# Row pairs for the upper half of the spectral weights, in a fused attention and spectral-mixing kernel

## The chip, the cores and the metric

The kernel runs on one core of a Trainium2 chip. The metric is the device time of one execution in microseconds, lower being better. TensorE (PE) multiplies matrices, with a separate unit that loads its weights (PEld); VectorE (DVE) and ScalarE (ACT) read PE's results from PSUM; GpSimd (POOL) here mainly issues transfers, and SyncE (SP) issues the stores of the output. Sixteen DMA engines carry out all transfers.

## The reference

The inputs are float32. `q`, `k` and `v` have 8 batches, 8 heads, 576 positions and 64 elements; `f` has one forget gate for each batch, head and position. Causal attention with a decay from the gates gives `x` of 8 x 576 x 512. Then the 64 lowest frequencies of `x` along the positions are multiplied by one complex 512 x 512 matrix per frequency ("mode"), and the result is transformed back and mixed.

```python
log_f = np.log(np.clip(f, 0.0001, 1.0)); cum = np.cumsum(log_f, axis=-1)
scores = scale * np.matmul(q, k.transpose(0, 1, 3, 2))
decay = cum[:, :, :, None] - cum[:, :, None, :]
attn = softmax(np.where(causal, -1000000000.0, scores + decay))
x = np.matmul(attn, v)            # then (B, S, H * D)
X = np.fft.rfft(x, axis=1)
Xr, Xi = (np.real(X[:, :n_modes]), np.imag(X[:, :n_modes]))
Yr = np.einsum('bmd,mde->bme', Xr, w_r) - np.einsum('bmd,mde->bme', Xi, w_i)
Yi = np.einsum('bmd,mde->bme', Xr, w_i) + np.einsum('bmd,mde->bme', Xi, w_r)
Y[:, :n_modes] = Yr + 1j * Yi
u = x + np.fft.irfft(Y, n=S, axis=1)
return u + np.maximum(u @ w_ch, 0.0)
```

`w_r` and `w_i` are 64 matrices of 512 x 512 each, 134 MB together, and all of them are read once.

## The kernel before

**Weights and units.** A unit is four modes (`NU` = 16 units). The 512 rows `d` of a unit's matrices come in four tiles, numbered by `dc`, each of 128 partitions and 1 MB in bf16. The transfers convert float32 to bf16, and so POOL issues them. For `dc` 0 and 1 a tile holds 128 rows (0 to 127, or 128 to 255) of both `w_r` and `w_i`, with one row on each partition; it is loaded in two halves, one for each of the two matrices (L156), and each contiguous run is one row of 512 numbers. For `dc` 2 and 3 a tile holds rows 256 to 511 of `w_r` (2) or `w_i` (3), with two neighbouring rows on each partition ("row pairs"), and a contiguous run is two rows (L165). `issue_w` loads the tiles in the order of `wseq`: first the list `early`, then the rest by unit. `issue_half` loads half a tile. Tiles lie in the pool `wpool` of seven buffers, used in turn, except for a few "guests" that lie in space of `x_all` or `yx` that is free at that time. A load waits until the product that read the buffer before has been computed.

**Two phases.** The first phase is a loop over 32 pairs of heads (`g` 0 to 3, and batch `b` within each), with two iterations more to drain it. Iteration `i` issues the loads of `q` and `k` for pair `i + 4`, half a weight tile, the load of `v` for pair `i + 3`, and another half tile (except where `i` is in `less`). Then PE, DVE and ACT work on the scores of pair `i` and on the values of pair `i - 1`: transposes of `q` and `k` (`tp`), scores (`sps`, `s`), transposes of the scaled values (`vn` on DVE, `tv`, `vT`, `vp`), products with the values (`pav`), and the normalization into `x_all`. The order of instructions on each engine is the order of the program (`manual_schedule`). At the end of iteration `i` stands `dft(i - 2)`, the spectrum of pair `i - 2`: five matmuls with the position blocks of `x_all` as weights and a basis of 3 x 64 columns (`bas3`). For `g` of 0 and 1 (pairs 0 to 15, iterations 2 to 17) the result is copied to `XS`, with one row `d` on each partition; for `g` of 2 and 3 it is two groups of five matmuls, with every second row as weights, and the result goes to `XP`, which has row pairs on the partitions.

**Early products.** From iteration 10, `spec_early` multiplies one tile of `early` by the spectrum, one at the end of each iteration and a second one in iterations 10 to 13. It takes eight matmuls into a PSUM tile `A0`, four at a time in different column groups. For `dc` 0 ACT copies the result to `yacc` in `yx`; for `dc` 1 DVE adds it there. `early` has 28 entries: `dc` 0 of all 16 units, then `dc` 1 of units 0 to 11. PSUM tiles with the tag `m` (transposes, spectrum, early products and others) take turns in two buffers.

**Second phase.** It goes through the units, with the tiles that are left (`dc` 2 and 3, and from unit 12 on `dc` 1 too). Each product frees a buffer, and POOL issues the next load after it. Beside this the kernel computes `x @ w_ch` (`pxw`), and folds the first 12 units back into `x` (`fold`). After the last tile the rest is folded, and the output is computed and stored.

The weight operands of the products are slices like these, for `dc` 0 and 1, and for 2 and 3:

```python
lhsT, rhs = XS[:, dc, c0 : c0 + 32], w8[:, n, j, :]
lhsT, rhs = XPv[:, c0 : c0 + M, m], w8[:, j, n, :]
```

## Time and profile before

| what | value |
|---|---|
| three runs, median (lowest to highest) | 437.75 us (437.21 to 437.8) |
| the profiled execution: its time, its span | 436.43 us, 434.6 us |
| PE, DVE, ACT, POOL busy | 343.3, 267.9, 234.1, 145.0 us |
| the loop's end (first product of the second phase) | 232.75 us |
| landing of the last weight tile | 402.1 us |
| 1024 KB load, issue to landing (median) | 29.5 us (`w_r`), 31.7 us (`w_i`) |
| 512 KB load, issue to landing (median) | 11.1 us (`w_r`), 12.3 us (`w_i`) |
| bytes read from HBM, written | 163.73 MB, 9.44 MB |

Times inside the execution are counted from the start of the span. The page cuts the span into 40 slices of 10.9 us; a digit is the busy share of a slice in tenths. The DMA row is the mean share of the 16 DMA engines. In the DMA view "share" is the sum of the packets' own times over 16 engines' time, and it is above 100 % when an engine has more than one packet under way. A row of a timeline has the start in us, the duration in us, the engine, the line, the operation with its tiles, the count, and in brackets the idle time before it and what ended it. A row of the chain of waits has the start, the duration, the engine, the tile, the line and the count.

### The profile page before, as it was taken

The numbers are of one execution on the slowest core, as the hardware profiler recorded it, in microseconds if no ns is written. First come the engines' busy times: TensorE is split into PE (matmuls) and PEld (weight loads), VectorE is DVE, ScalarE is ACT, GpSimd is POOL, SyncE is SP. The second block draws the span as 40 slices with busy tenths as digits, with TensorE's granted clock in tenths as the row PEclk, the third lists the DMA queues.
The fourth block names the chain that finished last, engine by engine and source line by source line (L and its number), as shares of the span: only waits on it lengthen the run. The fifth ranks groups of instructions, "written<-read, shape, count | busy, mean of one in ns | idle before, by whom it ended". The sixth has DMA issues, their size and how long they took to land.

```text
span 434.6 us, 10304 instructions
## 1 busy us (share of the span) xinstructions
PE 343.3 (79%) x4264; PEld 189.6 (44%) x4274; DVE 267.9 (62%) x651; ACT 234.1 (54%) x358; POOL 145.0 (33%) x215
## 2 busy tenths in 40 slices
PE   1689787798898898988896386599877498888993
PEld 1455555554555565555553142244433233334330
DVE  6677888877778778888885122222233165565794
ACT  4556777687887766656660022024322166564783
POOL 6544445444544353444213211111122202110273
PEclk9986999999999999999999579589999699999998
DMA  8999999999999999999999999999999999998498
GB/s 185 205 233 220 233 219 232 225 227 233 231 229 227 226 228 225 228 225 228 227 218 213 212 212 211 212 212 213 211 212 212 209 209 211 210 209 158 168 383 323
DMA packets 68543, 96.76 MB, mean 223 GB/s; under 512 B 3728, under 2 KB 45200, under 8 KB 68496
## 3 DMA queue, kind: packets, MB, share of 16 engines
q0 software_dynamic: 62800, 85.64, 106.3%
q1 hardware_dynamic: 5696, 10.47, 6.6%
q8 instruction: 33, 0.54, 0.4%
q14 instruction: 14, 0.11, 0.1%
HBM read 163.73 MB, written 9.44 MB: 398 GB/s over the span
## 4 chain that ended last, share of the span: by engine, by line
DMA 43%; PE 31%; DVE 18%; issue 3%; ACT 3%; POOL 1%; DVEq 0%; POOLq 0%
DMA w<-in_moe_w_r_dram 22%; DMA w<-in_moe_w_i_dram 20%; PE pav L477 5%; DVE vT L384 4%; DVE qkT L360 4%; DVE x_all L492 4%; PE A L194 4%; PE sps L432 3%; PE tv L382 3%; PE pd L521 3%; PE vp L393 2%; DMA qk<-in_k_dram 2%; PE Z L654 2%; DVE vn L372 2%; PE U L654 2%
## 5 line engine op out<-in xcount | busy, mean ns | idle before, releaser
L439 ACT ACTIVATE et<-sps 128x1024 bf16<-128x1024 f32 x96 | 96.0, 1049 | 13.9 <-PE sps L432 11.5
L477 PE MATMUL pav<-vs,et 128*128 128x65 bf16 (+1 forms) x896 | 52.1, 198 | 0.2 <-DVE vn L372 0.2
L360 DVE COPY qkT<-tp 128x640 bf16<-128x640 bf16 x64 | 48.7, 763 | 2.8 <-PE tp L355 2.8
L815 DVE TENSOR_TENSOR Yb<-A,yx 128x512 bf16<-128x512 f32 x15 | 10.4, 691 | 61.0 <-PE A L194 60.9
L477 PEld LDWEIGHTS <-et 128*128 128x128 bf16 (+1 forms) x896 | 37.2, 103 | 17.9 <-issue 13.6
L432 PE MATMUL sps<-qkT 64*128 64x512 bf16 (+4 forms) x320 | 39.8, 312 | 1.1 <-DVE qkT L360 1.1
L194 PE MATMUL A<-w,XP 128*16 128x512 bf16 (+1 forms) x240 | 21.9, 449 | 23.0 <-DMA w<-in_moe_w_i_dram 12.8
L694 PE MATMUL pxw<-wch,xT 128*128 128x512 bf16 (+1 forms) x152 | 39.0, 402 | 0.9 <-issue 0.3
L492 DVE TENSOR_TENSOR x_all<-pav,rcp 128x384 bf16<-128x384 f32 (+2 forms) x96 | 36.2, 377 | 3.3
L355 PE MATMUL tp<-ident_bf,qk 128*64 128x128 bf16 x576 | 30.3, 237 | 9.3 <-DMA qk<-in_k_dram 9.3
L384 DVE COPY vT<-tv 128x576 bf16<-128x576 bf16 x32 | 24.2, 757 | 19.8 <-PE tv L382 19.8
L165 POOL DMA_DIRECT2D w<-in_moe_w_r_dram x16 | 11.9, 743 | 71.8 <-PE A L194 50.5
L701 ACT CAST XW<-pxw 128x512 bf16<-128x512 f32 (+1 forms) x16 | 9.4, 585 | 47.3 <-PE pxw L694 47.3
L156 POOL DMA_DIRECT2D w<-in_moe_w_r_dram x27 | 20.5, 758 | 38.7 <-DMA w<-in_moe_w_i_dram 9.4
L404 ACT COPY vs<-vp 128x576 bf16<-128x576 bf16 x32 | 20.5, 640 | 21.7 <-PE vp L400 21.7
L165 POOL DMA_DIRECT2D w<-in_moe_w_i_dram x19 | 13.3, 698 | 53.3 <-PE A L194 31.6
L701 ACT CAST yx<-pxw 128x512 bf16<-128x512 f32 (+1 forms) x24 | 14.0, 585 | 31.4 <-PE pxw L694 31.4
L109 POOL DMA_DIRECT2D qk<-in_q_dram x32 | 19.5, 610 | 32.5 <-PE sps L432 6.2
L741 ACT CAST x_all<-pu 128x512 bf16<-128x512 f32 (+1 forms) x40 | 23.4, 584 | 11.2 <-PE pu L740 10.3
L491 DVE RECIPROCAL rcp<-pav 128x6 f32<-128x6 f32 (+2 forms) x96 | 16.2, 169 | 17.4 <-PE pav L477 17.3
L156 POOL DMA_DIRECT2D w<-in_moe_w_i_dram x27 | 20.3, 752 | 18.4 <-DMA w<-in_moe_w_i_dram 8.2
L109 POOL DMA_DIRECT2D qk<-in_k_dram x32 | 19.2, 601 | 19.3 <-DMA w<-in_moe_w_i_dram 5.2
(149 smaller groups left out, 677.8 us busy)
## 6 DMA issues: line engine op xcount, KB each, us to landing
w<-in_moe_w_r_dram POOLq DMA_DIRECT2D x16, 1024.0 KB, 29.5
w<-in_moe_w_i_dram POOLq DMA_DIRECT2D x15, 1024.0 KB, 31.7
w<-in_moe_w_r_dram POOLq DMA_DIRECT2D x27, 512.0 KB, 11.1
w<-in_moe_w_i_dram POOLq DMA_DIRECT2D x27, 512.0 KB, 12.3
out_dram<-o_sb SPq DMA_DIRECT2D x36, 256.0 KB, 3.2
vt<-in_v_dram POOLq DMA_DIRECT2D x29, 288.0 KB, 10.7
qk<-in_q_dram POOLq DMA_DIRECT2D x32, 144.0 KB, 10.8
qk<-in_k_dram POOLq DMA_DIRECT2D x32, 144.0 KB, 10.4
```

What stands on the lines that cost most here:

```text
L109: nc.gpsimd.dma_start(qk[64 * n : 64 * n + 64, :, :], src[b, 2 * g : 2 * g + 2, :, :].rearrange("h (p r) d -> p h (r d)", p=64),)
L156: nc.gpsimd.dma_start(w8[:, t, :, :], src[4 * u : 4 * u + 4, dc * 128 : (dc + 1) * 128, :].rearrange("m p e -> p m e"),)
L165: nc.gpsimd.dma_start(w8[:, j : j + step, :, :].rearrange("p m r e -> p m (r e)"), src[m : m + step, 256:512, :].rearrange("m (p r) e -> p ...
L194: nc.tensor.matmul(A[32 * j : 32 * j + M, :], lhsT=lhsT, rhs=rhs, start=st_, stop=sp_)
L355: nc.tensor.transpose(tp[64 * hp : 64 * hp + 64, r - r0, :, :].rearrange("p n c -> p (n c)"), qk[:, hp, r * 64 : r * 64 + 64], ident_bf[:, :],
L360: nc.vector.tensor_copy(st[i]["T"][:].rearrange("p n (c r) -> p n c r", r=9)[:, :, :, r0:r1], tp[:, 0 : r1 - r0, :, :].rearrange("p r n c ...
L384: nc.vector.tensor_copy(st[i]["vT"][:].rearrange("p (c r) -> p c r", r=9), tv[:].rearrange("p r c -> p c r"))
L432: nc.tensor.matmul(ps[:, hp, c : c + n], lhsT=KT[sl, jb * 128 : jb * 128 + 128], rhs=QT[sl, i0 : i0 + n], start=True, stop=True,)
L439: nc.scalar.activation(st[i]["et"][:, T, :, :], ps[:], ACT.Exp, scale=scale)
L477: nc.tensor.matmul(pav[:Ms, sb % 3, hp, :], lhsT=eblk(i, hp, jb, sb), rhs=rhs, start=(jb == 0), stop=(jb == sb),)
L492: nc.vector.tensor_tensor(x_all[:ns, g, b, lo:hi, :].rearrange("p s (h d) -> p s h d", h=2), pav[:ns, lo % 3 : lo % 3 + n, :, 0:Dh], _stri ...
L694: nc.tensor.matmul(pxw[rows, :], lhsT=xT[:, eb, sb * 128 : sb * 128 + Ms], rhs=wch[:, eb, :], start=(eb == 0), stop=(eb == NEB - 1),)
```

## The change

For units 8 to 15, the tiles of `dc` 0 and 1 take the form that `dc` 2 and 3 have: `dc` 0 is rows 0 to 255 of `w_r` and `dc` 1 the same rows of `w_i`, in row pairs on 128 partitions. Their contiguous runs in HBM are two rows, 4096 B in float32. Units 0 to 7 keep the old form (`by_rows`). Halves of the new tiles are two modes each; in the second phase such a tile is one transfer.

The spectrum of rows 0 to 255 is therefore made in two forms: for the modes of units 0 to 7 as before into `XS` (now half as long), and for the modes of units 8 to 15 by row pairs into the new tile `XQ`. For pairs 0 to 15 `dft` issues three groups of five matmuls with 96 columns each, in place of one group with 192, and two ACT copies in place of one.

Because `dc` 0 of a unit from 8 on needs the spectrum of all 16 pairs of `g` 0 and 1, the order of `early` changes: `dc` 0 of units 0 to 7, `dc` 1 of units 0 to 7, then `dc` 0 of units 8 to 15 and `dc` 1 of units 8 to 11. The second product per iteration stands in iterations 10, 11, 18, 19 and 20, and iteration 16 has none. Tiles 16 and 17 of the sequence (units 8 and 9, `dc` 0) become guests in `yx`.

```diff
--- before.py
+++ after.py
@@ -50,7 +50,9 @@
     KL = 2 * NM - KF
     NW = 7
     NX = 12
-    XROW = 24 * NM + 32
+    NL = 8
+    ML = 4 * NL
+    XROW = 24 * ML + 32
     scale = 1.0 / math.sqrt(Dh)
     TWO_PI_OVER_S = 2.0 * math.pi / S
     NEAREST = 1.5 * 2.0**23
@@ -66,6 +68,7 @@
     x_all = const.tile([128, NEB, B, NSB, 128], BF16, name="x_all")
     XS = const.tile([128, 2, XROW], BF16, name="XS")
     XP = const.tile([128, 2, 24, NM], BF16, name="XP")
+    XQ = const.tile([128, 2, 24, NM - ML], BF16, name="XQ")
     wch = const.tile([128, NEB, D], BF16, name="wch")
     ident_bf = const.tile([128, 128], BF16, name="ident_bf")
     ident_f = const.tile([128, 128], F32, name="ident_f")
@@ -122,7 +125,8 @@
         )
 
 
-    early = [(u, 0) for u in range(NU)] + [(u, 1) for u in range(NX)]
+    early = [(u, dc) for dc in range(2) for u in range(NL)]
+    early += [(u, 0) for u in range(NL, NU)] + [(u, 1) for u in range(NL, NX)]
     wseq = early[:]
     for u in range(NU):
         wseq += ([] if (u, 1) in early else [(u, 1)]) + [(u, 2), (u, 3)]
@@ -135,7 +139,13 @@
         4: yx[:, 6:8, :].rearrange("p k e -> p (k e)").bitcast(BF16),
         6: yx[:, 4:6, :].rearrange("p k e -> p (k e)").bitcast(BF16),
         11: x_all[:, 3, :, :, :].rearrange("p b s c -> p (b s c)"),
+        16: yx[:, 4:6, :].rearrange("p k e -> p (k e)").bitcast(BF16),
+        17: yx[:, 6:8, :].rearrange("p k e -> p (k e)").bitcast(BF16),
     }
+
+    def by_rows(u, dc):
+
+        return dc < 2 and u < NL
 
     def issue_w(half=None):
         n = wissued[0]
@@ -144,19 +154,29 @@
         u, dc = wseq[n]
         if half != 1:
             if n in guests:
-                w8 = guests[n][:, 0 : 8 * D].rearrange("p (t m e) -> p t m e", t=2, m=4)
+                t = 2 if by_rows(u, dc) else 4
+                w8 = guests[n][:, 0 : 8 * D].rearrange("p (t m e) -> p t m e", t=t, e=D)
             else:
-                shape = [128, 2, 4, D] if dc < 2 else [128, 4, 2, D]
+                shape = [128, 2, 4, D] if by_rows(u, dc) else [128, 4, 2, D]
                 w8 = wpool.tile(shape, BF16, tag="w8", name="w8")
             wtile[(u, dc)] = w8
         w8 = wtile[(u, dc)]
-        if dc < 2:
+        if by_rows(u, dc):
             for t, src in enumerate((moe_w_r, moe_w_i)):
                 if half in (None, t):
                     nc.gpsimd.dma_start(
                         w8[:, t, :, :],
                         src[4 * u : 4 * u + 4, dc * 128 : (dc + 1) * 128, :].rearrange("m p e -> p m e"),
                     )
+        elif dc < 2:
+            src = (moe_w_r, moe_w_i)[dc]
+            step = 4 if half is None else 2
+            for j in range(2 * (half or 0), 4 if half != 0 else 2, step):
+                m = 4 * u + j
+                nc.gpsimd.dma_start(
+                    w8[:, j : j + step, :, :].rearrange("p m r e -> p m (r e)"),
+                    src[m : m + step, 0:256, :].rearrange("m (p r) e -> p m (r e)", r=2),
+                )
         elif half != 1:
             src = (moe_w_r, moe_w_i)[dc - 2]
             step = 1 if n + 1 == len(wseq) else 4
@@ -176,6 +196,14 @@
         whalf[0] ^= 1
 
     XPv = XP[:].rearrange("p r c m -> p (r c) m")
+    XQv = XQ[:].rearrange("p r c m -> p (r c) m")
+
+    def by_pair(dc, c, n, m):
+
+        c0 = 24 * c + (8 if dc % 2 == 0 else 0)
+        if dc < 2:
+            return XQv[:, c0 : c0 + n, m - ML]
+        return XPv[:, c0 : c0 + n, m]
 
     def spec_mms(A, u, dc, first, last):
         w8 = wtile.pop((u, dc))
@@ -183,14 +211,13 @@
             for j in range(4):
                 m = 4 * u + j
                 st_, sp_ = first and n == 0, last and n == 1
-                if dc < 2:
+                if by_rows(u, dc):
                     M = 32
                     c0 = m * 24 + (8 if n == 0 else 0)
                     lhsT, rhs = XS[:, dc, c0 : c0 + 32], w8[:, n, j, :]
                 else:
                     M = 32 if st_ else 16
-                    c0 = 24 * n + (8 if dc == 2 else 0)
-                    lhsT, rhs = XPv[:, c0 : c0 + M, m], w8[:, j, n, :]
+                    lhsT, rhs = by_pair(dc, n, M, m), w8[:, j, n, :]
                 nc.tensor.matmul(
                     A[32 * j : 32 * j + M, :], lhsT=lhsT, rhs=rhs, start=st_, stop=sp_
                 )
@@ -202,12 +229,7 @@
             for eb in range(NEB):
                 for n in range(2):
                     m = 4 * u + j
-                    if dc < 2:
-                        c0 = m * 24 + (8 if n == 0 else 0)
-                        lhsT, rhs = w8[:, n, j, eb * 128 : (eb + 1) * 128], XS[:, dc, c0 : c0 + 16]
-                    else:
-                        c0 = 24 * n + (8 if dc == 2 else 0)
-                        lhsT, rhs = w8[:, j, n, eb * 128 : (eb + 1) * 128], XPv[:, c0 : c0 + 16, m]
+                    lhsT, rhs = w8[:, j, n, eb * 128 : (eb + 1) * 128], by_pair(dc, n, 16, m)
                     nc.tensor.matmul(
                         AT[:, eb, 2 * j : 2 * j + 2, :].rearrange("p c b -> p (c b)"),
                         lhsT=lhsT,
@@ -313,7 +335,7 @@
         nc.vector.tensor_copy(bas3[:, :, 2, :], Zt[:, :, :, 1])
 
     def setup_late():
-        nc.vector.memset(XS[:, :, 24 * NM : XROW], 0.0)
+        nc.vector.memset(XS[:, :, 24 * ML : XROW], 0.0)
         nc.vector.tensor_copy(
             perm[:].rearrange("p (b j ri) -> p b j ri", b=8, j=4),
             ident_bf[:].rearrange("p (j x ri b) -> p b j x ri", j=4, x=2, ri=2)[:, :, :, 0, :],
@@ -499,18 +521,26 @@
     def dft(i):
         g, b = pairs[i]
         if g < 2:
-            pd = psM.tile([128, 3, NM], F32, tag="m", name="pd")
-            for sc in range(NSB):
-                ns = SBLK[sc]
-                nc.tensor.matmul(
-                    pd[:],
-                    lhsT=x_all[:ns, g, b, sc, :],
-                    rhs=bas3[:ns, sc, :, :],
-                    start=(sc == 0),
-                    stop=(sc == NSB - 1),
-                )
+            pd = psM.tile([128, 3, 3, ML], F32, tag="m", name="pd")
+            half = slice(64 * g, 64 * g + 64)
+            for r in range(3):
+                for sc in range(NSB):
+                    ns = SBLK[sc]
+                    xs = x_all[:ns, g, b, sc, :]
+                    nc.tensor.matmul(
+                        pd[half, r, :, :] if r else pd[:, 0, :, :],
+                        lhsT=xs[:, r - 1 : 128 : 2] if r else xs,
+                        rhs=bas3[:ns, sc, :, ML:NM] if r else bas3[:ns, sc, :, 0:ML],
+                        start=(sc == 0),
+                        stop=(sc == NSB - 1),
+                    )
             nc.scalar.copy(
-                XS[:, g, 0 : 24 * NM].rearrange("p (m c b) -> p c m b", c=3, b=8)[:, :, :, b], pd[:]
+                XS[:, g, 0 : 24 * ML].rearrange("p (m c b) -> p c m b", c=3, b=8)[:, :, :, b],
+                pd[:, 0, :, :],
+            )
+            nc.scalar.copy(
+                XQ[half, :, :, :].rearrange("p r (c b) m -> p r c b m", c=3)[:, :, :, b, :],
+                pd[half, 1:3, :, :],
             )
             return
         pd = psM.tile([128, 2, 3, NM], F32, tag="m", name="pd2")
@@ -601,7 +631,7 @@
             scale_v(i + 1)
         if i == 1:
             setup_basis()
-        if 10 <= i < 14:
+        if i in (10, 11, 18, 19, 20):
             spec_early(*early[spec_done])
             spec_done += 1
         if i >= 2:
@@ -614,7 +644,7 @@
             setup_bi4(0, 512)
         if i == 4 + NSB:
             setup_bi4(512, 64)
-        if i >= 10:
+        if i >= 10 and i != 16:
             spec_early(*early[spec_done])
             spec_done += 1
     actx.close()
```

## The prediction

> **What bounds the kernel now.** I read the 40 slices first, then the chain of waits, then the DMA queues in three windows, and last the timelines of the engines around one iteration. From the page:
>
> ```profile
> PE   1689787798898898988896386599877498888993
> DMA  8999999999999999999999999999999999998498
> GB/s 185 205 233 220 233 219 232 225 227 233 231 229 227 226 228 225 228 225 228 227 218 213 212 212 211 212 212 213 211 212 212 209 209 211 210 209 158 168 383 323
> DMA 43%; PE 31%; DVE 18%; issue 3%; ACT 3%; POOL 1%; DVEq 0%; POOLq 0%
> ```
>
> The DMA row is full from the second slice to the 36th (about 10 to 395 us). The chain runs over engines up to 202 us, then over weight loads until the last one lands at 402.1, and 32.5 us of computation follow. So two clocks run side by side: the loads, which never stop, and the attention loop (to 232.8), which frees the weight buffers that later loads need. The end is the time of the loads plus the tail, as long as the loop does not starve them. What a packet costs comes from the DMA view of three windows: 100 to 200, 240 to 330 and 345 to 390 us:
>
> ```profile
> DMA packets 19467, 22.72 MB, mean 227 GB/s; under 512 B 1116, under 2 KB 18546, under 8 KB 19452
> q0 software_dynamic: 19452, 22.50, 120.8%
> ...
> DMA packets 9570, 19.07 MB, mean 212 GB/s; under 512 B 291, under 2 KB 291, under 8 KB 9565
> q0 software_dynamic: 9565, 18.99, 111.9%
> ...
> DMA packets 6315, 9.45 MB, mean 210 GB/s; under 512 B 191, under 2 KB 3240, under 8 KB 6313
> q0 software_dynamic: 6313, 9.42, 116.0%
> ```
>
> A packet is counted at its size in bf16, so a row of weights is one of 1024 B and a row pair one of 2048 B. Of the loop I use the chain of waits from 113 to 124 us and around 146 us:
>
> ```profile
> 113.88 0.62 PE pd L505 x5
> 114.50 0.55 PE A L194 x8
> 115.05 0.32 PE sps L432 x2
> 115.37 0.29 PE pav L477 x6
> 115.66 0.32 PE sps L432 x4
> 116.00 0.49 PE tv L382 x18
> 116.51 0.76 DVE vT L384
> ...
> 146.11 1.18 PE pd L521 x10
> ```
>
> Here the spectrum (pd) and the early product (A) are on the path: PE goes through them to the transposes tv, and DVE waits for those.
>
> **The change, part by part.** *Packets.* Sixteen weight tiles (units 8 to 15, two each) go from 1024 packets of 1024 B to 512 of 2048 B. In 240 to 330, 16 engines x 90 us over 9274 packets is 155.3 ns for 2048 B. In 345 to 390, 720 us less 3073 x 155.3 ns leaves 79.6 ns for each of 3049 packets of 1024 B. A pair saves 2 x 79.6 - 155.3 = 3.9 ns; 512 pairs over 16 engines are 0.125 us a tile. In 100 to 200, 27 weight loads give 13824 packets of 1024 B, q and k 3606 of 1152 B (1.125 times as dear, by bytes), v 906 of 4608 B (at 175 ns, my estimate above the 2048 B price); 1600 us then gives 80.6 ns, 5.9 ns a pair and 0.189 us a tile. Twelve of the tiles load in that stage, four after 310 us: 12 x 0.189 + 4 x 0.125 = 2.8 us, G. If a 2048 B packet is dearer in the loop by the same share, all sixteen save 0.125, 2.0 us; if v packets cost only 155 ns, 3.5. That the packet size is worth nothing is the first rival. Issuing costs POOL no more: a half tile takes 0.76 us for 512 rows, and will have 256; the four late tiles go in one issue in place of two.
>
> *Spectrum.* In 16 iterations (2 to 17) 5 matmuls with 192 columns (0.62 us) become 15 with 96. By columns that is 0.62 x 1.5 = 0.93 us; by count, at the 0.118 us of L521, 1.77. I take 1.20: L521, two groups of five, costs 0.59 us a group, and each of five matmuls is about 40 ns shorter (the 65-column av products run at 0.43 us for 10). So d = 0.58 us more PE work per iteration, between 0.31 and 1.15. The Trainium skill, "TensorE: Matmul & The Clock Gate", section "Wait — 56ns, not 53.3ns?", has back-to-back matmuls start N / 2.4 GHz + 2.5 ns apart: by it 15 matmuls would take 0.64 us and d would be 0.02. The row pd L505 is against it, 0.62 us where the rule gives 0.41.
>
> The ACT copy of 128x192 (1.04 us) becomes one of 128x96, about 0.55 by half, and one of 64x192, about 0.25 by the 0.47 us that 64x384 takes: less than before. The smaller memset and the weights read from XQ lie beside other work; if not, 8 products of L194 took 0.55 us with XS and 1.11 for 16 with XP, the same.
>
> *What d costs, S.* Iterations 2 to 9 have no product, and tv waits 0.42 us for DVE's vn at 81.83, behind a basis matmul of 0.14: cover 0.56. If it is gone, all of d above 0.56 counts; here 0.02 x 8 = 0.2 us. Iterations 10 and 11 keep two products: +0.58 each. 12 and 13 lose one product, worth 0.60 by the step from 6.95 to 6.35 us: nothing. 14, 15 and 17 take d whole: 1.74. 16 loses its only product: nothing. Iterations 18 to 20 get a second one, now of the second quarter, which DVE adds (L546, 0.68 us). DVE comes to it only after vn: in the iteration at 207 us it adds from 209.70 to 210.38. The second product needs that product's PSUM buffer (two in turn, the spectrum has the other), so it starts at 210.38 and ends at 210.93, where the scores now start at 209.27: +1.66 each, 5.0 in all (0.6 each if the add were free earlier). S = 0.2 + 1.16 + 1.74 + 5.0 = 8.1 us, and 17.2 with d = 1.15.
>
> *Does S reach the loads?* In iterations 29 to 33 each load waits for a product to free its buffer:
>
> ```profile
> 223.12 0.74 POOL L165 DMA_DIRECT2D w<-in_moe_w_i_dram  x1 [4.84 <-PE sps L432]
> 228.38 0.74 POOL L165 DMA_DIRECT2D w<-in_moe_w_r_dram  x1 [4.51 <-PE A L194]
> ...
> DMA to landing us min/median/max: 19.4/19.5/19.7
> ```
>
> Of the 19.4 us of the load issued at 228.38 its own transfer takes 4.97 (512 packets x 155.3 ns / 16), and the first packet of the run starts 2.2 us after its issue by the packets' own times; 0.3 us end it. Slack 11.9 us. S uses 8.1, and the loads ahead come 2.3 us earlier (12 x 0.189): 10.4. The queue does not run dry, with 1.5 us to spare.
>
> An earlier pinch is the load at 121.28: its buffer is that of the eighth product, which moves from iteration 13 to 15 and ends at 121.40 + 2.5 = 123.9. POOL stands 2.6 us; behind it stand the v load, the other half and the next q and k. A load lands some 11 us after its issue, so the transfers under way cover it; uncovered it would be 2.6 us at most. The new guests let units 8 and 9 load without a wpool buffer.
>
> After the loop PE comes 8 us later to its first product (232.75), and waits there for loads 22.0 us up to 345, so it catches up; without that the end would be 8 us later. From 342 to 402 it waits for loads about 2 us in all, so PE can follow G.
>
> **Sum.** -2.8 us. The profiled execution took 436.43 us (span 434.6 and 1.8 around it), 1.3 under the median of 437.75; that 436.43 goes to 433.6, the median to 435.0.
>
> **The rivals.** *1. Bytes, not packets, set the loads.* The reads are 4096 B per 2048 B packet: 9274 x 4096 B / 90 us = 422 GB/s, and 412 with 79.6 ns per 2048 B: near each other, which speaks for it; against it are two windows with the dearer small packet. Then G = 0 and the time stays 437.7. The Trainium skill, "HBM Reference", section "Specifications (TRN2)", has a core that streams alone at about 425 GB/s, bounded by its 16 DMA engines; by that figure 3 % at most is left in these tiles. The trace agrees with 422.
>
> *2. The loop starves the loads (the other side).* Place: the buffer waits at 217 to 231 us. S = 16 d - 1.2, so with S + 2.3 - 11.9 lost, it begins at d = 0.68 and eats all of G at d = 0.86, that is at 1.48 us for 15 matmuls. At d = 1.15 it loses 17.2 + 2.3 - 11.9 = 7.6 us: 437.75 - 2.8 + 7.6 = 442.5. For it: L521's ten matmuls cost nearly twice L505's five, so the count weighs. Against: columns shrink by half.
>
> *3. The change gains more:* if pairs save 9 ns, as they would if q, k and v packets were cheaper than bytes say, G is 4.6 and the time 433.2.
>
> **How the numbers follow.** A difference of 0.2 % (0.9 us) is about what a measurement can tell here. Forecast 0.52 (433.7 to 436.5, G from 2.0 to 3.5 less a little starving): 0.49 faster, 0.03 same. Rival 1 0.16: 0.05 faster, 0.08 same, 0.03 slower. Rival 2 0.27 (of which beyond 440.8 about 0.1): 0.03 faster, 0.02 same, 0.22 slower. Rival 3 0.05, faster. Together 0.62, 0.13, 0.25. The range runs from 433.0 to 440.8; the forecast alone has 433.7 to 436.5.
>
> **What would show it.** Right: q0 has about 8190 packets fewer; the pd rows sum to 1.2 us an iteration; iterations 18 to 20 take about 8.4 us; the loop ends near 241; the DMA row stays full, and the last load lands near 399. Wrong, if DMA share falls below 1.0 anywhere from 120 to 245 us, if the loop ends after 245, or if 345 to 390 moves no more than 210 GB/s with pairs alone; also if PE's half clock, seen at 340 to 350 (0.51), falls in the last 50 us, where PE has 2 us to spare.

## The result, and the profile after

The changed kernel is slower: its time is 1.0071 times the time before, with an interval from 1.0045 to 1.0097. The median of 22 executions is 443.02 us (436.9 to 450.04), against 436.82 us (435.75 to 438.22) of 22 executions before. Executions of the changed kernel spread over 3 % and go with the mean granted clock (0.953 where it took 436.9 us, 0.890 where it took 449.56); the ratio takes those within 1.5 % of the fastest, and the profile is of a slower one, of 445.75 us. Over all executions the medians lie 1.4 % apart. The prediction was 435.0 us, with a range from 433.0 to 440.8: it came out slower where faster was forecast, and its median lies above the range.

The page of the changed kernel, cut like that of before, with the row of the granted clock, one queue, and the group in which PE waits for q and k:

```profile
PE   1679899898989887988889787399889398889993
PEclk9998768959999999999999999589969779999997
DMA  8999999999998999999999999999999999999498
GB/s 188 205 233 221 229 221 230 233 199 223 203 177 147 235 223 236 223 237 223 237 226 190 193 211 212 212 212 212 212 212 212 212 212 212 212 212 180 173 381 301
...
q0 software_dynamic: 54544, 85.63, 102.1%
...
DMA 39%; PE 34%; DVE 12%; issue 9%; ACT 3%; POOL 2%; DVEq 0%; POOLq 0%
...
L377 PE MATMUL tp<-ident_bf,qk 128*64 128x128 bf16 x576 | 31.1, 242 | 10.0 <-DMA qk<-in_k_dram 10.0
```

The queue carries the same 85.6 MB in 8256 packets fewer (62800 before). But GB/s falls to 177 and 147 in the two slices from 122 to 144 us, and to 190 and 193 in those from 233 to 255; before, every slice from the third to the 36th was at 209 or more. PEclk, in tenths, lies between 5 and 8 in five of the slices from 33 to 100 us. Stretches in which the granted clock is 0.50 are called half clock from here on. The same in windows; the columns are the window, its length, then busy time and instructions of PE, PEld, DVE, ACT and POOL, the granted clock, the DMA share and GB/s. Before:

```profile
40.00:120.00 80.00, 66.32 (x1168) 43.68 (x1164) 64.62 (x179) 61.27 (x84) 36.83 (x57) 1.00 1.21 228
120.00:140.00 20.00, 17.32 (x307) 11.24 (x304) 15.98 (x46) 15.79 (x22) 9.21 (x15) 1.00 1.21 229
220.00:260.00 40.00, 27.54 (x295) 14.06 (x295) 16.70 (x46) 9.12 (x16) 7.43 (x10) 0.79 1.13 212
```

After:

```profile
49.80:63.30 13.50, 13.18 (x155) 8.12 (x156) 8.23 (x21) 7.42 (x12) 6.62 (x11) 0.50 1.21 228
40.00:120.00 80.00, 73.23 (x1078) 48.12 (x1072) 56.08 (x157) 49.61 (x78) 33.02 (x51) 0.81 1.20 223
120.00:140.00 20.00, 17.49 (x312) 11.74 (x311) 14.73 (x40) 15.36 (x24) 9.60 (x15) 1.00 0.79 145
220.00:260.00 40.00, 34.16 (x560) 21.57 (x557) 29.48 (x81) 19.11 (x29) 8.92 (x12) 1.00 1.09 205
```

The loads lose 20 x (1 - 145/229) = 7.3 us in 120 to 140 and 40 x (1 - 205/212) = 1.3 us in 220 to 260; another 80 x (1 - 223/228) = 1.8 us goes in 40 to 120, 10.4 us together. With what the pairs gain, the last weight tile lands 9.1 us later, at 411.2 us (402.1 before); the loop ends at 251.8 (232.8 before). So the loop is 19.0 us late, 2.3 times the predicted 8.1, and 34.1 us of it, between 36 and 101 us, run at half clock. The profile of before has one such stretch too, from 29.0 to 39.3 us; it began ahead of the first matmul of the spectrum (34.7 us), and at 38 us the two loops are level. The loop was hardly held up by its own loads: PE waited 10.0 us for q and k in the whole execution, 9.3 before.

What POOL waits for where the queue runs dry, in the timeline of POOL:

```profile
120.95 0.74 POOL L167 DMA_DIRECT2D w<-in_moe_w_r_dram  x1 [6.23 <-PE A L221]
...
134.88 0.77 POOL L167 DMA_DIRECT2D w<-in_moe_w_r_dram  x1 [9.45 <-PE A L221]
```

Two loads stand for 6.23 and 9.45 us until an early product has freed their buffer, and the loads behind them, of q, k and v too, stand with them.

The steps of one iteration, from the chain of waits (start, duration, engine, tile, line, count); the first is at half clock:

```profile
95.44 1.97 PE pd L530 x15
...
118.78 1.31 PE pd L530 x15
...
146.10 1.33 PE pd L530 x15
147.45 0.61 ACT XS L537
148.10 0.61 PE A L221 x8
...
150.09 0.76 DVE vT L406
...
158.22 0.76 DVE vT L406
```

The 15 matmuls take 1.31 to 1.33 us at full clock. At 147.45 stands a wait that was not there before: the product of iteration 17 is the first to need the spectrum made just ahead of it, and PE waits for its copy. The distance of the last two rows, 8.13 us, is an iteration with two products.

### The profile page after: what moved, and what is told of

The parts are those of the page before. It is cut to its first block, busy times and chain, and to the rows that moved or that the text cites. A ratio compares the mean times of both kernels' runs of the same rounds, so it can differ in the third digit from the quotient of the medians.

```text
span 444.0 us, 10660 instructions
## 1 busy us (share of the span) xinstructions
PE 363.1 (82%) x4434; PEld 203.9 (46%) x4434; DVE 269.2 (61%) x651; ACT 232.7 (52%) x374; POOL 141.5 (32%) x211
## 4 chain that ended last, share of the span: by engine, by line
DMA 39%; PE 34%; DVE 12%; issue 9%; ACT 3%; POOL 2%; DVEq 0%; POOLq 0%
DMA w<-in_moe_w_i_dram 29%; DMA w<-in_moe_w_r_dram 7%; PE pd L530 5%; PE pav L499 5%; PE sps L454 5%; DVE vT L406 4%; DVE qkT L382 3%; PE A L221 3%; DVE x_all L514 3%; PE tv L404 3%; PE vp L415 2%; DMA qk<-in_k_dram 2%; PE pd L551 2%; PE Z L684 2%; PE U L684 1%
## 5 line engine op out<-in xcount | busy, mean ns | idle before, releaser
L461 ACT ACTIVATE et<-sps 128x1024 bf16<-128x1024 f32 x96 | 93.8, 1025 | 19.9 <-PE sps L454 18.8
L499 PE MATMUL pav<-vs,et 128*128 128x65 bf16 (+1 forms) x896 | 54.0, 202 | 0.2 <-DVE vn L394 0.2
L499 PEld LDWEIGHTS <-et 128*128 128x128 bf16 (+1 forms) x896 | 38.7, 105 | 19.3 <-issue 15.4
L454 PE MATMUL sps<-qkT 64*128 64x512 bf16 (+4 forms) x320 | 42.1, 330 | 1.2 <-DVE qkT L382 1.1
L845 DVE TENSOR_TENSOR Yb<-A,yx 128x512 bf16<-128x512 f32 x15 | 10.4, 691 | 53.6 <-PE A L221 53.5
L185 POOL DMA_DIRECT2D w<-in_moe_w_r_dram x16 | 11.9, 746 | 75.8 <-PE A L221 69.3
L221 PE MATMUL A<-w,XP 128*16 128x512 bf16 (+1 forms) x240 | 20.9, 433 | 15.3 <-DMA w<-in_moe_w_i_dram 8.8
L426 ACT COPY vs<-vp 128x576 bf16<-128x576 bf16 x32 | 20.5, 640 | 22.2 <-PE vp L422 22.2
L731 ACT CAST yx<-pxw 128x512 bf16<-128x512 f32 (+1 forms) x24 | 14.0, 585 | 34.1 <-PE pxw L724 34.1
L185 POOL DMA_DIRECT2D w<-in_moe_w_i_dram x19 | 13.3, 701 | 53.1 <-PE A L221 37.8
L771 ACT CAST x_all<-pu 128x512 bf16<-128x512 f32 (+1 forms) x40 | 23.4, 584 | 11.2 <-PE pu L770 10.3
L377 PEld LDWEIGHTS <-qk 128*64 128x64 bf16 x576 | 20.2, 119 | 14.0 <-issue 9.3
L394 DVE TENSOR_TENSOR vn<-vt,wn 128x576 bf16<-128x576 f32 x32 | 23.8, 744 | 1.9 <-ACT wn L319 1.9
L724 PEld LDWEIGHTS <-xT 128*128 128x128 bf16 (+1 forms) x160 | 14.9, 103 | 20.6 <-issue 5.8
## 6 DMA issues: line engine op xcount, KB each, us to landing
w<-in_moe_w_r_dram POOLq DMA_DIRECT2D x23, 512.0 KB, 11.2
w<-in_moe_w_i_dram POOLq DMA_DIRECT2D x19, 512.0 KB, 10.8
vt<-in_v_dram POOLq DMA_DIRECT2D x29, 288.0 KB, 10.4
qk<-in_k_dram POOLq DMA_DIRECT2D x32, 144.0 KB, 10.1
```

Source lines behind the costliest of these rows:

```text
L185: nc.gpsimd.dma_start(w8[:, j : j + step, :, :].rearrange("p m r e -> p m (r e)"), src[m : m + step, 256:512, :].rearrange("m (p r) e -> p ...
L221: nc.tensor.matmul(A[32 * j : 32 * j + M, :], lhsT=lhsT, rhs=rhs, start=st_, stop=sp_)
L377: nc.tensor.transpose(tp[64 * hp : 64 * hp + 64, r - r0, :, :].rearrange("p n c -> p (n c)"), qk[:, hp, r * 64 : r * 64 + 64], ident_bf[:, :],
L394: nc.vector.tensor_tensor(vn[:], st[i]["vt"][:], _strided(wn[:, widx(i), :], [[1, 9], [0, Dh]]), ALU.mult)
L454: nc.tensor.matmul(ps[:, hp, c : c + n], lhsT=KT[sl, jb * 128 : jb * 128 + 128], rhs=QT[sl, i0 : i0 + n], start=True, stop=True,)
L461: nc.scalar.activation(st[i]["et"][:, T, :, :], ps[:], ACT.Exp, scale=scale)
```

## Experiments

Two explanations were tested against each other: that the loop is late by the work that the change adds and moves (theory 1 in the expectations), or that half clock makes it late, which the prediction had not counted at all (theory 3). Theory 2 is that row pairs are no faster than rows. Each part was also run alone. A ratio is again against the kernel before. How late the loop is at an iteration is read from the start of its `vT` copy, against the profile of before.

**The changed kernel again.** No edit.

> The changed kernel once more, for a second profile. Theory 1 (the loop is late, so the loads dry up): a ratio of about 1.007 again, POOL's waits for early products near 120 and 134 us (6.2 and 9.5 us in the first profile) come again, shorter where the granted clock stays higher, and the DMA share falls below 1.0 in 120 to 140 us by as much as those waits exceed some 8 us of transfers under way. Theory 2 (row pairs are no faster than rows, or slower): a full DMA row and the same time all the same. Theory 3 (the spectrum of 15 short matmuls lets the granted clock fall to a half in the loop, and the loop is late for that alone): half-clock stretches between 40 and 112 us as in the first profile, and a time that goes with the granted clock.

Ratio 1.0066 [1.0044, 1.0088], from two of six executions, which took 439.83 to 448.02 us; in the profile, of 447.24 us, the loop ends at 251.4 and the last tile lands at 411.8. Two later profiles of it, beside other experiments:

> The changed kernel a third time, for one more profile: theory 3 expects half-clock stretches before 112 us wherever the time is above 440 us, few where it is below; theory 1 expects the same waits of POOL for products at the same places, the longer the later the loop.

> The changed kernel a fourth time, for a profile of an execution that shows a higher granted clock. Theory 3: with few half-clock stretches before 112 us the DMA share stays above 1.0 at 120 to 140 us and the time is 436 to 439 us.

Two executions each: 443.8 and 447.75 us (ratio 1.0199 [1.0159, 1.0239]), 446.09 and 449.14 us (1.023 [1.0182, 1.0277]). The loop ends at 250.8 and 251.1, with half clock in the first 101 us in both. In 120 to 140 us the DMA share is 0.91, 0.91 and 0.82 in these three profiles. The last profile was to have a higher clock; its mean is 0.916. So a profile with the loop near 251 us, half clock ahead of it and a dry queue near 130 us is what this kernel usually does. None of its four profiles shows the loop at full clock, so its fastest executions (436.9 us) were not seen from inside.

**The transfers alone.** Pairs are loaded as in the change, and the products take them with the old spectrum, whose rows are not paired.

```diff
+                    w8[:, j : j + step, :, :].rearrange("p m r e -> p m (r e)"),
+                    src[m : m + step, 0:256, :].rearrange("m (p r) e -> p m (r e)", r=2),
...
-                    lhsT, rhs = XS[:, dc, c0 : c0 + 32], w8[:, n, j, :]
+                    lhsT = XS[:, dc, c0 : c0 + 32]
+                    rhs = w8[:, n, j, :] if by_rows(u, dc) else w8[:, j, n, :]
```

> The kernel before with the transfers alone changed: units 8 to 15 have rows 0 to 255 in row pairs, the spectrum, the order and the products' shapes stay (so the products of these tiles multiply the wrong rows). Theory 1: faster by 2.0 to 3.5 us, ratio 0.992 to 0.996, a full DMA row, loop end at 232.8 as before. Theory 2: ratio 0.998 to 1.005, and the end of the last load no earlier than 402. Theory 3: as theory 1.

0.9958 [0.9944, 0.9972], 435.22 us (434.81 to 436.08). That is as theories 1 and 3 have it (0.992 to 0.996); theory 2 is ruled out. The last tile lands at 400.4, 1.7 us earlier than before. G is 1.7 to 1.8 us, by the medians and by the ratio. The loop ends 1.7 us earlier too (231.1), but that is not the pairs: 1.6 us of it is there by 38 us, since this profile has no half clock from 29 to 39 us. The DMA view of 345 to 390 us:

```profile
DMA packets 4788, 9.53 MB, mean 212 GB/s; under 512 B 147, under 2 KB 147, under 8 KB 4786
```

Where before moved 210 GB/s with rows and pairs mixed, pairs alone move 212.

**The order alone.** The new `early`, the two guests and the moved products, with rows and the old spectrum.

```diff
-    early = [(u, 0) for u in range(NU)] + [(u, 1) for u in range(NX)]
+    early = [(u, dc) for dc in range(2) for u in range(NL)]
+    early += [(u, 0) for u in range(NL, NU)] + [(u, 1) for u in range(NL, NX)]
...
-        if 10 <= i < 14:
+        if i in (10, 11, 18, 19, 20):
...
-        if i >= 10:
+        if i >= 10 and i != 16:
```

> The kernel before with the order alone changed: the new list of early products with second products in iterations 10, 11, 18, 19 and 20, and the two new guests; transfers by rows and the old spectrum stay. Theory 1: POOL waits at about 121 us for the eighth product, 1 to 3 us; iterations 18 to 20 take 8.1 to 8.5 us; loop end 3 to 5 us later than 232.8; the loads stay busy; ratio 0.998 to 1.003. Theory 2: the same. Theory 3: the granted clock stays at about 0.94.

1.0007 [0.9995, 1.0019]. The loop ends at 236.6, 3.8 us later, and the queue stays full; the wait of POOL near 121 us did not come (0.4 us). By the `vT` copies of the trace, iterations 12 and 13 save 1.2 us together, iteration 17 loses 1.1 (the new wait), and each of iterations 18 to 20 loses 1.3.

**The spectrum alone.** 15 matmuls and `XQ`, with rows and the old order; the upper units multiply row pairs of the spectrum by single rows.

```diff
-            pd = psM.tile([128, 3, NM], F32, tag="m", name="pd")
+            pd = psM.tile([128, 3, 3, ML], F32, tag="m", name="pd")
...
+            for r in range(3):
...
+                        lhsT=xs[:, r - 1 : 128 : 2] if r else xs,
+                        rhs=bas3[:ns, sc, :, ML:NM] if r else bas3[:ns, sc, :, 0:ML],
```

> The kernel before with the spectrum alone changed: 15 matmuls of 96 columns, two ACT copies, XS and XQ; transfers by rows and the old order of the early products stay (the products of units 8 to 15 take their weights from XQ though their tiles hold rows, and partly from an XQ that isn't filled yet, so what they compute is not the reference's). Theory 1: the loop is later by 8 x (0.70 - 0.56) + 8 x 0.70 = 6.7 us with the 1.32 us that the first profile has for 15 matmuls, within the slack of 11.9 us: ratio 0.998 to 1.003. Theory 2: the same. Theory 3: half-clock stretches between 40 and 112 us, the loop 10 to 20 us late, ratio over 1.005.

1.0113 [1.006, 1.0165], from two of six executions; all six lie between 439.37 and 459.52 us. The range from 0.998 to 1.003 was missed; theory 3's "over 1.005" was right. The profile, of 459.52 us, in windows:

```profile
60.00:80.00 20.00, 19.32 (x264) 12.50 (x264) 13.35 (x37) 11.90 (x19) 8.54 (x14) 0.66 1.21 231
...
140.00:160.00 20.00, 17.34 (x214) 10.70 (x212) 10.55 (x28) 10.62 (x16) 5.92 (x10) 0.59 0.96 159
160.00:180.00 20.00, 18.80 (x258) 11.28 (x250) 10.83 (x29) 11.62 (x17) 6.84 (x12) 0.69 0.94 159
```

With nothing moved, the queue runs dry as well, at other places: the granted clock is 0.59 to 0.69, the loop ends at 263.4 and the last tile lands at 423.8. But this kernel is later than the change, and for a reason of its own. The view of waits from 100 to 160 us (what waits, for what, the sum in us, how often, the longest):

```profile
PE A L210 <- ACT XQ L531: 4.0, 4, 1.0
```

In the old order the products of iterations 14 to 17 read `XQ` while it is still being filled, so PE waits for its copy four times; in the change only iteration 17 has such a wait. At iteration 11 the loop is 11.2 us late, as in the change; iterations 14 to 18, with these waits and most of the half clock, add 17.4 us. So it shows that the 15 matmuls bring half clock and a dry queue without the other parts, and it does not give their price in the change. That the three parts come near the whole (-0.42 + 0.07 + 1.13 = +0.78 % against +0.71 measured) proves nothing for the same reason.

**As much PE work in wide matmuls.** Five matmuls of 320 columns into spare space, beside the old spectrum, in the same iterations.

```diff
+            for _ in range(5):
+                nc.tensor.matmul(
+                    pdw[:, 3 * NM : 512],
+                    lhsT=ident_bf[:, :],
+                    rhs=x_all[:, g, b, 0:3, :].rearrange("p s c -> p (s c)")[:, 0:320],
+                    start=True,
+                    stop=True,
+                )
```

> The kernel before with five more matmuls of 128 x 128 weights and 320 columns in the spectrum of pairs 0 to 15 (their result is used by nothing): some 0.67 us more PE work in each of iterations 2 to 17, as much as the 0.70 that the 15 short matmuls add, but in wide matmuls. Theory 1 (PE's longer loop alone delays the loads): the time of the kernel with the new spectrum alone, ratio 1.006 to 1.017 among comparable runs. Theory 3 (the short matmuls lower the granted clock, and that delays the loop): the granted clock stays at 0.93 or above with no half-clock stretch between 40 and 200 us, the loop is 5 to 8 us later, inside the slack, and the ratio is 0.998 to 1.003.

1.0008 [0.9998, 1.0018]. The loop ends at 241.6, 8.8 us late, which is inside the slack, and the clock stays full:

```profile
40.00:120.00 80.00, 69.12 (x1154) 46.36 (x1151) 61.44 (x168) 56.61 (x78) 36.77 (x57) 1.00 1.21 228
```

So the added work alone does not bring half clock, and 8.8 us of lateness cost nothing that could be measured in the time (the last tile lands at 403.1, 1.0 us later).

**The layout changed once.** The old spectrum with 5 matmuls; the upper modes are put into row pairs once, in iterations 18 to 21.

```diff
+                nc.tensor.matmul(
+                    sh[64 * g : 64 * g + 64, r, :],
+                    lhsT=ident_bf[:, r:128:2],
+                    rhs=XS[:, g, lo : lo + 192],
...
+        nc.scalar.copy(XS[:, :, lo : lo + 192], sh[:])
...
+        if 18 <= i < 22:
+            shuffle(i - 18)
```

> The changed kernel with the spectrum of before (5 matmuls of 192 columns, all 64 modes into XS), and the upper 32 modes brought into row-pair form once, by 16 matmuls with columns of the identity and four ACT copies in iterations 18 to 21; transfers, order and guests as changed. Theories 1 and 3 (the spectrum is what costs, be it by its time or by the clock): the gain of the row pairs alone remains, ratio 0.994 to 0.998, loop end 236 to 240, no half-clock stretch between 50 and 200 us. Theory 2 (something else of the combination costs): ratio above 1.002.

0.999 [0.9967, 1.0013], 434.66 to 440.14 us: above the expected 0.994 to 0.998, and the expected loop end (236 to 240) and full clock were missed too. In the profile a new wait of PE, and a window near the loop's end:

```profile
133.68 1.04 PE L220 MATMUL A<-w,XS 128*32 128x512 bf16 x8 [1.13 <-ACT XS L533]
```

```profile
230.00:240.00 10.00, 9.08 (x148) 5.89 (x150) 8.66 (x26) 6.67 (x11) 0.74 (x1) 1.00 0.96 162
```

The loop ran at full clock until 133.0 us, then at half clock for 17.1 us; it ends at 245.1, and the queue has a dry spot at 230 to 240. So half clock can come in this loop without the 15 matmuls, here from the iteration on that begins the second half of the pairs and the new matmuls on the layout. Without the 15 matmuls the loss is gone, but a gain is not sure: the interval holds no change, and in this profile the loop still ends late.

**Fewer products moved.** Second products stay in iterations 12 and 13, and iterations 14 to 16 have none.

```diff
-        if i in (10, 11, 18, 19, 20):
+        if i in (10, 11, 12, 13, 18, 19, 20):
...
-        if i >= 10 and i != 16:
+        if i >= 10 and i not in (14, 15, 16):
```

> The changed kernel with second early products in iterations 10, 11, 12, 13, 18, 19 and 20, and none in 14 to 16: units 0 to 7 of the first quarter are done by iteration 13 as in the kernel before, so their buffers come free two iterations earlier. Theory 1: POOL's waits near 120 and 134 us go, the DMA share stays above 1.1 from 110 to 150 us, and the ratio falls from 1.007 to 0.998 to 1.004; half-clock stretches before 112 us may come all the same. Theory 3 alone (the clock costs the time wherever the buffers stand): ratio 1.005 to 1.010.

1.0161 [1.0133, 1.0188], four executions; the changed kernel's two on the same chip gave 1.0199. If the moved products were the cause, 0.998 to 1.004 was due: missed. The range for half clock alone, 1.005 to 1.010, was missed as well, on the other side. The windows:

```profile
120.00:140.00 20.00, 17.04 (x299) 12.35 (x299) 16.20 (x45) 14.50 (x23) 9.92 (x16) 1.00 1.19 230
230.00:240.00 10.00, 9.12 (x168) 6.03 (x167) 7.91 (x21) 7.28 (x11) 1.48 (x2) 1.00 0.83 136
```

The dry place at 120 to 140 is gone, and the queue is dry at 230 to 240 instead. The loop still ends at 246.6, with half clock at 35, 48 and 69 us, 20.5 us in all. In these two profiles the moved products only choose where a late loop starves the loads.

**More work on top of the change.** Five matmuls of 224 columns in the iterations with the spectrum.

```diff
+            for _ in range(5):
+                nc.tensor.matmul(
+                    pdw[:, 9 * ML : 512],
+                    lhsT=ident_bf[:, :],
+                    rhs=x_all[:, g, b, 0:2, :].rearrange("p s c -> p (s c)")[:, 0:224],
```

> The changed kernel with five more matmuls of 128 x 128 weights and 224 columns in the spectrum of pairs 0 to 15 (their result is used by nothing), some 0.5 us more PE work in each of iterations 2 to 17. Theory 3 in the form that PE's clock falls because the short matmuls of 64 weight columns keep the array too little at work: the half-clock stretches before 112 us go or become fewer, and the kernel is no slower than the changed one in spite of the added work, ratio 0.998 to 1.006. Theory 1 (PE's time alone): slower than the changed kernel by the slack that is used up, ratio 1.012 or more.

1.0182 [1.0146, 1.0218]. The expectation of 0.998 to 1.006, that keeping PE's clock up would take the loss away, was missed; 1.012 or more was right. The windows and POOL:

```profile
40.00:120.00 80.00, 71.02 (x1197) 50.40 (x1197) 58.17 (x160) 52.01 (x83) 35.82 (x56) 1.00 1.21 226
120.00:140.00 20.00, 17.63 (x298) 12.53 (x297) 13.62 (x40) 13.02 (x22) 8.01 (x13) 1.00 0.89 160
```

```profile
131.98 0.76 POOL L167 DMA_DIRECT2D w<-in_moe_w_r_dram  x1 [10.22 <-PE A L221]
```

The clock is full in this profile (its mean over an execution is 0.943 to 0.962 in five of six, 0.891 in the sixth, of 462.84 us). The loop ends at 249.8 all the same, by work alone, and the queue runs dry at the same place as in the changed kernel. Lateness does the harm, wherever it comes from.

**The change's time without its short matmuls.** The spectrum is made by the old five matmuls of 192 columns and five more of 320 (1.31 us together, as in the change); `XQ` is filled with the unpaired rows.

```diff
+            for _ in range(5):
+                nc.tensor.matmul(
+                    pdw[:, 3 * NM : 512],
+                    lhsT=ident_bf[:, :],
...
-                pd[half, 1:3, :, :],
+                pd[half, :, :].rearrange("p c (r m) -> p r c m", r=2),
```

> The changed kernel (transfers, order, guests, two ACT copies) with a spectrum that is as long on PE but made of wide matmuls: the 5 of 192 columns of the kernel before and 5 of 320 columns whose result nothing uses, about 1.3 us in all (so XQ gets the spectrum of single rows, and the products of units 8 to 15 are not the reference's). The clock and PE's work are told apart: if the longer work alone (11 us over 16 iterations) delays the loads, then with a granted clock of 0.94 and no half-clock stretch before 130 us the DMA share falls below 1.1 at 120 to 140 us and the ratio is 1.004 or more. If it takes the half-clock stretches, the share stays above 1.1 there, the loop ends near 243, and the ratio is 0.996 to 1.002.

1.0025 [1.0002, 1.0048], 435.73 to 440.5 us, just above the 0.996 to 1.002 expected if half clock is the cause; the loop end near 243 and the share above 1.1 came as expected. The spectrum of one iteration in the chain, then the windows:

```profile
88.62 0.79 PE pdw L528 x5
89.41 0.52 PE pdw L537 x5
```

```profile
40.00:120.00 80.00, 69.87 (x1155) 46.99 (x1154) 62.01 (x172) 55.41 (x90) 36.74 (x57) 1.00 1.21 228
120.00:140.00 20.00, 16.83 (x282) 11.34 (x274) 15.66 (x43) 14.12 (x22) 9.03 (x14) 1.00 1.17 222
220.00:260.00 40.00, 34.34 (x461) 19.67 (x453) 24.36 (x65) 15.78 (x25) 7.91 (x11) 0.91 1.10 203
```

The wait of POOL that was 9.45 us in the change, and the `vT` copy of iteration 11 before, here, and in the change:

```profile
126.10 0.76 POOL L167 DMA_DIRECT2D w<-in_moe_w_r_dram  x1 [4.93 <-PE A L221]
...
89.29 0.76 DVE vT L384
...
91.85 0.76 DVE vT L406
...
100.57 0.76 DVE vT L406
```

The same PE time and order as in the change, at full clock: the loop ends at 242.9, 10.1 us late, and the last tile lands at 402.3. The gain of the pairs is used up (0.9958 to 1.0025), but the 19 us of lateness and the landing at 411.2 are not there. At the `vT` copy of iteration 11 this kernel is 2.6 us later than before, the changed kernel 11.3: the half clock ahead of 101 us is worth the 8.7 us between (7.7 to 8.7 in its four profiles). Little else of the short matmuls shows there: where its clock is full, an iteration of the changed kernel between the third and the ninth takes 6.6 to 6.8 us (here 6.4 to 6.7), and one wholly at half clock takes 9.27 us (52.3 to 61.5). From iteration 11 to the loop's end, nearly all at full clock in both, they lose the same, about 7.6 us.

**A version that keeps the gain.** The layout changed once, second products in iterations 10 to 13 and 18 to 21 and none in 14 to 17, each second product issued ahead of the iteration's last mask and `vn` on DVE.

```diff
+        if i in (10, 11, 12, 13, 18, 19, 20, 21):
+            spec_early(*early[spec_done])
+            spec_done += 1
         if live:
...
-        if i >= 10 and i != 16:
+        if i >= 10 and i not in (14, 15, 16, 17):
```

> The kernel with the spectrum of before and the shuffle, with second early products in iterations 10 to 13 and 18 to 21 and none in 14 to 17, and the second one issued before DVE's masks and vn, so that its DVE add comes ahead of them. Theory 3, with the loop's lateness as what the clock acts through: no wait of the product of iteration 17 for the spectrum just made (1.13 us in the shuffle's profile), the loop ends 2 to 5 us earlier than the shuffle's 245, the loads stay busy at 220 to 240 us, ratio 0.994 to 0.998. If the gain of the row pairs is eaten elsewhere: 0.999 or more.

0.996 [0.9943, 0.9977], 435.76 us (434.76 to 436.7), as expected: faster than both kernels, and as fast as the transfers alone.

```profile
120.00:140.00 20.00, 15.05 (x277) 10.42 (x276) 16.25 (x45) 14.28 (x19) 9.04 (x15) 1.00 1.19 230
230.00:240.00 10.00, 9.93 (x158) 6.00 (x154) 6.92 (x22) 4.42 (x8) 2.28 (x4) 1.00 1.09 195
```

The loop ends at 239.1, the clock is full from 41 to 242 us, and the last tile lands at 400.5.

**All profiles together.** The second rival of the prediction gives a landing for each loop end: lateness is free up to 11.9 us (loop end 244.7), or 9.6 us (242.4) where pairs bring the loads 2.3 us ahead, and then counts whole. From there on, 402.1 without pairs and 400.4 with them:

| kernel | loop end | last landing | by the rival |
|---|---|---|---|
| before | 232.8 | 402.1 | 402.1 |
| the transfers alone | 231.1 | 400.4 | 400.4 |
| the order alone | 236.6 | 401.6 | 402.1 |
| a version that keeps the gain | 239.1 | 400.5 | 400.4 |
| as much PE work in wide matmuls | 241.6 | 403.1 | 402.1 |
| the change's time without its short matmuls | 242.9 | 402.3 | 400.9 |
| the layout changed once | 245.1 | 403.9 | 403.1 |
| fewer products moved | 246.6 | 407.5 | 404.6 |
| more work on top of the change | 249.8 | 408.5 | 407.8 |
| the change (first profile) | 251.8 | 411.2 | 409.8 |
| the spectrum alone | 263.4 | 423.8 | 420.8 |

It is never more than 3.0 us off, over a spread of 23 us, whatever made the loop late. So the rival and its slack were right to about 3 us; what the forecast put into it was not. Its place was only part of the story: in the change more was lost at 120 to 140 us than at the loop's end. Each row is one profile.

## Why the prediction was wrong

- **The step that failed** is S, the loop's lateness: "S = 8.1 us", and with it "The queue does not run dry, with 1.5 us to spare". It measured 19.0 us. Two terms were missing or too small.
- **Half clock, 8.7 us, was not a term at all.** The prediction took full clock for the whole loop and looked for half clock in the last 50 us alone. The two kernels with the same PE time, short and wide matmuls, differ by these 8.7 us already at iteration 11, and by 8.9 at the loop's end. By the rival's own formula 10.1 us would have cost 0.5 us of landing; 19.0 cost 9.4 us (measured, beyond the transfers alone: 1.9 and 10.8 us). By the ratios the 10.1 us cost more, 0.9958 to 1.0025, which is 2.9 us.
- **d, 0.58 predicted, is 0.70 measured** (1.31 to 1.33 us for 15 matmuls, 0.62 for 5). The estimate by groups of five was closer than columns alone (0.93 us). The Trainium skill's rule of N / 2.4 GHz + 2.5 ns ("TensorE: Matmul & The Clock Gate", "Wait — 56ns, not 53.3ns?") would have had 0.64 us, and d = 0.02; the trace disagrees. With d = 0.70 the prediction's S = 16 d - 1.2 is 10.0, and at full clock the loop was 10.1 us late. That the sum is so near is partly luck, as the next point shows.
- **Terms of S**, read at full clock in the kernel with wide matmuls, where d is 0.70 too. Iterations 3 to 9 lost 1.8 us; the cover of 0.56 us would have left 1.0, so the cover was less. Iterations 10 and 11 lost 0.55 each, 12 and 13 nothing, 14 and 15 0.6 each and 16 nothing, all near the forecast. Iteration 17 lost 1.4 us: its wait for its own spectrum, 1.1 us in the order alone, was overlooked. Iterations 18 to 20 take 8.13 us, predicted about 8.4, and lost 3.9 us together, predicted 5.0. The second product there waited for ACT's copy of the spectrum (0.48 us at 155.70), not for DVE's add, so the mechanism was another one and the price near. What was too low and what was too high cancel.
- **The pinch at 121 us** was predicted at "2.6 us at most", covered by the transfers under way. POOL stood 0.4 us there in the order alone, 4.93 at full clock with wide matmuls, and 9.45 in the change. The forecast took the loop to be 2.5 us late at that point; it was 1.2 us early, 3.7 late and 12.5 late in these three (iteration 15). As a place it was right, and the one where most was lost; but taking the pinch away moved the loss to 230 to 240 us.
- **G** was put at 2.8 us (2.0 to 3.5); it measured 1.7 to 1.8, a little below the range's end. The late rate was right (in 345 to 390, 16 x 45 us over 4786 - 147 packets is 155.2 ns, predicted 155.3); even at the late rate alone all sixteen tiles would have saved 2.0 us, so the gain leaves no room for the dearer small packet of 100 to 200 us. The first rival, no gain at all, is wrong too.
- **The ACT copies** take 0.60 us and 0.31 to 0.61 (0.46 in the mean), not 0.55 and 0.25, so together no less than the 1.04 before; they lie beside other work except in iteration 17.
- **Signs of failure.** Two of those named came true: DMA share below 1.0 in 120 to 245 us (0.79), and a loop end after 245. Rival 2, with a chance of 0.27, was right about the mechanism and the sign; its price came from d alone, and at full clock that is a fraction of what was lost.

What stays open: why 15 short matmuls bring half clock. That they do in this loop is shown by the profiles with and without them: between 42 and 130 us there is half clock in all six of kernels with the 15 matmuls and no wide ones beside them, and in none of the seven without the 15. More work beside the same 15 matmuls kept the clock full in one profile, so being short is not enough by itself; and half clock at 133 us in the layout changed once, or at 29 us in the kernel before, came without them. Whether the fastest executions of the changed kernel simply escaped half clock was not seen in a profile, only in their mean clock.

## What to carry to other kernels

Where loads never stop, each load waits for a consumer to free its buffer, so price any delay of that consumer, by added work, by a reordering or by a lower clock, against the slack of the loads that wait for it, at each place where one waits, and read the slack from their issue and landing. Change a layout once, when its data are complete, rather than in every iteration of a loop whose clock has to stay full. When two versions have the same PE time on paper, the granted clock can still tell them apart, so run the new instructions in their own shape, not only their sum.

## What the runs showed that was not expected

**Half clock in a busy loop.** In the first profile of the changed kernel a stretch of 13.7 us began at 49.7 us although PE was busy 18.41 of the 20 us from 40 to 60 (12.43 of the 13.7 us just ahead of it), and no idle gap of PE between 30 and 50 us was over 1.01 us. The Trainium skill, "TensorE: Matmul & The Clock Gate", section "HAM oscillation — how this bites in real kernels", has as its rule that PE should not idle for more than about 3.4 us; by that rule no half clock was due here, and the trace does not agree. Nor does it in the kernel before, where the longest idle gap between 24 and 50 us is 1.14 us and a window near the first spectrum has a granted clock of 0.54:

```profile
30.00:40.00 10.00, 9.68 (x125) 6.20 (x125) 7.88 (x24) 5.22 (x7) 4.18 (x7) 0.54 1.21 236
```

The section after it, "A second HAM failure mode: psum-queue depth-cycling", has short idle times between groups of matmuls that make the clock swing; no run here isolates that. In the records the stretches inside an execution last 3.4, 6.8, 10.2, 13.7, 17.1 and once 20.5 us, steps of about 3.41 us.

**The clock's row can miss a stretch.** In the second profile of the changed kernel the window of 40 to 49 us has full clock:

```profile
40.00:49.00 9.00, 8.68 (x102) 5.51 (x98) 5.30 (x16) 4.64 (x7) 3.65 (x6) 1.00 1.22 220
```

But the chain of the same profile has the durations of half clock in it, 0.54 us for four `sps` matmuls (0.32 at full clock) and 1.97 for the spectrum:

```profile
40.33 0.54 PE sps L454 x4
...
43.96 1.97 PE pd L530 x15
```

The records of the clock begin at 49.9 us in this trace, and what lies ahead of them is shown as full clock. So the matmuls' own durations are to be read beside the row; in the kernels with wide matmuls they show no half clock between 40 us and the loop's end.
